# Shared logits groups, FFN column blocks of two and three, later tanh buffers and a new planned order in an attention-and-FFN kernel on one core

## The chip, the cores and the metric

The kernel runs on one core of one Trainium2 chip. The metric is the device time of one launch in microseconds (us). A core has five engines with their own instruction queues, each worked through in order: TensorE (PE, matrix products; its weight loads are shown as PEld), VectorE (DVE), ScalarE (ACT), GpSimd (POOL) and SyncE (SP, here the queue that issues nearly all DMAs). Matrix products write to PSUM, which the kernel holds as one tile `ps` of eight banks of 512 f32 columns; ACT and VectorE read them from there.

## The reference

2048 tokens of width 448, 16 heads of width 28, four segments of 512 tokens. Inside a segment attention is causal; what earlier segments hold comes in through a state M and a normaliser z. After it comes a gated FFN of width 1792. Both halves sit in residual branches with a layer norm, and a conditioning vector gives shifts, scales and gates.

```python
for s in range(N):                       # N = 4 segments of L = 512
    logits = einsum('bhqd,bhkd->bhqk', qs, ks) * scale + mask      # causal
    a_dot = einsum('bhqk,bhkd->bhqd', softmax(logits), vs)
    a_mem = (phi(qs) @ M) / (phi(qs) @ z + 1e-06)
    outs.append(g * a_mem + (1.0 - g) * a_dot)
    M = M + einsum('bhld,bhle->bhde', phi(ks), vs); z = z + sum(phi(ks))
...
mod = (silu(c) @ w_mod).reshape(...)     # sa, ca, ga, sb, cb, gb
h = layernorm(x) * (1 + ca) + sa
x = x + ga * A(h)                        # attention, then @ wo
h = layernorm(x) * (1 + cb) + sb
x = x + gb * ((sigmoid(h @ w_gate) * (h @ w_up)) @ w_down)
```

## The kernel before

**Stages.** The kernel runs once over four segments. For each one: a first layer norm and its transposition (`ln1`), the q, k and v products (`proj`, L665 and L686, evicted by ACT at L673 and L690), attention in four units of four heads each, the state update (`memory`), the output projection with residual and second norm (`wo_ln2`), and the FFN (`ffn`). Work of different segments overlaps.

**One attention unit.** Four heads lie in four quarters of PE's rows, so four products of 28 rows run side by side ("R" mode). The keys are taken in four blocks of 128; because of the causal mask block kb needs only the queries from kb x 128 on, 512, 384, 256 and 128 columns. They are gathered into three logits groups, each in four PSUM banks, one bank per head: block 0 (512 columns), blocks 1 and 3 (384 + 128), block 2 (256, half-filled). ACT makes one exponential of each group into the buffer `pT` (L755), POOL zeroes the upper triangle of each diagonal block (L761), and the product with v (L769, "C" mode, 32 columns of PE per head) accumulates all four blocks. There are two `pT` buffers; a unit takes one with its first logits group and gives it up after L769. After it come 32x32 transposes and normalisation on VectorE (L776 to L817). From segment 1 on the state's product (L783) is added; phi(q) and phi(k) start with an exponential on ACT (L697). phi(k) is transposed by a DMA (L708) and goes into the state product of `memory` (L714).

**The second norm.** L831 multiplies by wo (whose columns are scaled by ga beforehand), VectorE adds it to x (L835), takes statistics, POOL computes the reciprocal deviation (L574), VectorE normalises (L582), four DMAs transpose (L592), and ACT and VectorE apply shift and scale (L602, L605). Then the FFN of that segment can start.

**The FFN.** Width 1792 is 14 columns of 128. For each column, gate and up products go into a bank each. The contraction over 448 rows has three chunks of 128 and one of 64. A column taken alone makes 8 full-array matmuls, its last chunk padded with zeros. In a block of two columns the 64-row chunks of gate and up run side by side in the upper and lower half of PE's rows (L856, "R" mode): the first column's three chunks, the half-height products of both columns, then the second column's three chunks, which go on accumulating. Segment 0 takes 14 columns alone, the others 7 blocks of two (`REST`). ACT takes tanh of the gate into `tt` (L882, two buffers), VectorE combines it with up (L885) into one of 18 `fT` buffers; then L895 multiplies by w_down, whose 14 blocks were scaled by gb before (L551; blocks from `wdd` on by POOL, the others by VectorE).

**Order.** Nothing is issued in the order in which it is written. Every piece of work is a node with an engine, an estimated duration, dependencies, buffers it takes and uses, and a priority. `Graph.run` plays the nodes through with these estimates: at each moment every free engine takes the ready node of highest rank plus priority whose buffers are free, and the order found is what is emitted into the queues. A switch of PE's mode (`mode`: F whole array, R and C divided) costs the plan 100 ns. `Graph.fill` puts dummy matmuls (L930, L933) where the plan has PE idle in the first 90 us. `PRM` holds the priorities; the planned slot of a node decides its place, while on the chip only real dependencies and buffer releases are waited for.

Of the kernel before, what the change touches and what calls it, by code (L numbers as in the profile page):

```python
# [13 lines left out]
P = 128  # L14
# [4 lines left out]
FILL = 450  # L19


PRM = dict(T0=5000, STEP0=-1500.0, STEP=10000.0, lg=76000, ex=15000, mask=49000, wo=79000, tanh=-15500,
           up=81000, f=175500, dn=-495800, phi=-82000, t=-80000, ln1_1=-17000, ln1_2=-57000, ln1_3=-52000,
           mem=-32000, pj_0=36000, pj_1=5000, pj_2=-43000, pj_3=9000, ot=399000, stall=300, wds=-42000,
           wos=144000, wdd=6, mod=-26000, a0=99000, w0=-36000, stay=120000)


class Slot:
# [16 lines left out]
class Graph:  # L45
# [24 lines left out]
        return n  # L70

    def ready_at(self, n):
        t = n.release
        if n.move is not None and len(self.landed) >= LANES:
            t = max(t, self.landed[-LANES])
        for d in n.deps:
            t = max(t, d.end + d.lag + (self.LAG[d.eng][n.eng] if d.eng in self.LAG else 0))
        return t

    def ranks(self):  # L80
# [29 lines left out]
    def run(self):  # L110
# [3 lines left out]
        avail = {e: [] for e in ENGINES}  # L114
        for n in self.nodes:
            if not n.deps:
                avail[n.eng].append(n)
        at = dict.fromkeys(ENGINES, 0.0)
        mode = None
# [3 lines left out]
        while done < len(self.nodes):  # L123
            moved = False
            for e in ENGINES:
                if at[e] > t:
                    continue
                ready = sorted((n for n in avail[e] if self.ready_at(n) <= t), key=lambda n: -(n.rank + n.prio + (PRM["stay"] if e == "PE" and n.mode != "F" != mode else 0)))
                narrow = None
                for n in ready:  # L130
                    if n.lock is not None and self.port - t - n.lock > PRM["stall"]:
                        continue
                    got = self.place(n, t, narrow)
                    if got is None:
                        if narrow is None and any(s.width > 1 for s in n.take):
                            free = self.free["bank"]
                            narrow = min((0, 1), key=lambda h: sorted(free[4 * h:4 * h + 4], reverse=True))
                        continue
                    for s, i in zip(n.take, got):
                        s.at, s.t0 = i, t  # L140
                        for w in range(s.width):
                            self.free[s.pool][i + w] = float("inf")
                    extra = 0
                    if e == "PE":
                        extra = SWITCH if n.mode != mode else 0
                        mode = n.mode
                    n.start = t
                    if n.lock is not None:
                        extra = max(0.0, self.port - t - n.lock)
                    n.end = t + n.dur + extra  # L150
                    if n.lock is not None:
                        self.port = n.end
                    at[e] = n.end
                    if n.move is not None:
                        self.ring = max(self.ring, n.end) + n.move
                        n.lag = self.ring - n.end + LAND
                        self.landed.append(n.end + n.lag)
                    avail[e].remove(n)
                    order.append(n)
                    done += 1  # L160
                    for s in {id(x): x for x in (*n.take, *n.use)}.values():
                        if all(u.end is not None for u in s.users):
                            f = max(u.end + (u.lag if u.move is not None else 0) for u in s.users) + 120
                            for w in range(s.width):
                                self.free[s.pool][s.at + w] = f
                            if s.pool == "bank":
                                s.t1 = f
                                self.used.append(s)
                    for o in n.outs:
                        left[id(o)] -= 1  # L170
                        if left[id(o)] == 0:
                            avail[o.eng].append(o)
                    moved = True
                    break
            if moved:
                continue
            times = [x for x in at.values() if x > t]
            times += [r for e in ENGINES for n in avail[e] if (r := self.ready_at(n)) > t]
            times += [x for x in (self.port - PRM["stall"], self.port) if x > t]
            times += [x for x in self.landed if x > t]  # L180
            times += [f for fs in self.free.values() for f in fs if t < f < float("inf")]
            assert times, "the graph cannot go on"
            t = min(times)
# [24 lines left out]
def kernel(  # L208
# [31 lines left out]
    EPS = 1e-5  # L240
    OFF = (0, L, 2 * L, 2 * L - P)
    PTW = 2 * L + 2 * P
    KB_GROUPS = ((0,), (1, 3), (2,))
    NWARM = 12
    MOD_ACT = ((1, 3), (1, 3))

    REST = ((1,) * 14, (2,) * 7, (2,) * 7, (2,) * 7)
    NXN, NH, NQ, NV, NPT, NFT = 6, 3, 3, 3, 2, 18

    x_dram = A_x[0]  # L250
# [476 lines left out]
            rm_n[(s + 1, hc)] = dve(260, lambda hc=hc, rm=rm: nc.vector.tensor_tensor(  # L727
                rm_r[:, rm.at, :], M_sb[:, hc, :], bmask[:, s, :], ALU.mult), [u, n_bmask], take=[rm], lock=0, prio=PRM["mem"])

    def attention(s, hc, oT, release, prev):  # L730
        q, k, v = qT_of[s], kT_of[s], vt_of[s]
        pT = Slot("pT")
        a0 = 0 if s else PRM["a0"]
        masks = []
        for g, kbs in enumerate(KB_GROUPS):
            lg = Slot("bank", 4)
            w0 = OFF[kbs[0]]
            wid = sum(L - kb * P for kb in kbs)

            def mm(kbs=kbs, lg=lg):  # L740
                o = 0
                for kb in kbs:
                    nq = L - kb * P
                    for hs in range(4):
                        r = slice(HP * hs, HP * hs + Dh)
                        nc.tensor.matmul(ps[:, lg.at + hs, o:o + nq], lhsT=kT_r[r, k.at, hc, kb * P:(kb + 1) * P],  # L746
                                         rhs=qT_r[r, q.at, hc, kb * P:L], start=True, stop=True,
                                         tile_position=(HP * hs, 0))
                    o += nq
            n = add("PE", 230 if wid == L else 120, mm, [q_n[(s, hc)], k_n[(s, hc)], *lg_prev],  # L750
                    take=[lg, pT] if g == 0 else [lg], use=[q, k], release=release(g), mode="R", prio=PRM["lg"] + a0)
            lg_n.setdefault((s, hc), n)

            def ex(lg=lg, w0=w0, wid=wid):
                nc.scalar.activation(pT_r[:, pT.at, :, w0:w0 + wid], ps[:, lg.at:lg.at + 4, 0:wid], AF.Exp, scale=scale)  # L755
            e = act(1765 if wid == L else 920, ex, [n], use=[lg, pT], prio=PRM["ex"] + a0)
            lg_prev[:] = [n, e]
            for kb in kbs:
                def mask(kb=kb):
                    blk = pT_r[:, pT.at, :, OFF[kb]:OFF[kb] + P]  # L760
                    nc.gpsimd.affine_select(out=blk, in_=blk, compare_op=ALU.is_ge, fill=0.0, base=0,  # L761
                                            pattern=[[0, 4], [1, P]], channel_multiplier=-1)
                masks.append(pool_op(610, mask, [e], prio=PRM["mask"] + a0, use=[pT], lock=0))
        acc, A, R, O = bank(), Slot("A"), Slot("R"), Slot("O")

        def pv():
# [76 lines left out]
    def ffn(s, hT, hs):  # L843
# [15 lines left out]
        for size in REST[s]:  # L859
# [6 lines left out]
            for i, f in enumerate(fcs):  # L866
                if i == lead:
                    n_rest = gu_prev[0] = add("PE", size * 216, lambda fcs=fcs, bs=bs, lead=lead: rest(fcs, bs, lead),
                                              [gu_prev[0]], take=[x for g in fcs[lead:] for x in bs[g]],
                                              use=[hT, *(x for g in fcs[:lead] for x in bs[g])], mode="R",  # L870
                                              prio=PRM["up"])
                for j, (w_sb, loads, other) in enumerate(((wg_sb, lg_, tts[f]), (wu_sb, lu_, fs[f]))):
                    late, b = i >= lead, bs[f][j]
                    n = gu_prev[0] = add("PE", (4 if whole else 3) * 216,
                                         lambda w_sb=w_sb, b=b, f=f, whole=whole, late=late: half(w_sb, b, f, whole, late),
                                         [*hs, *loads, *n_gpad, gu_prev[0]], take=[other] if late else [b, other],
                                         use=[hT, b] if late else [hT], mode="F", prio=PRM["up"] * j)
                    done[f, j] = n
            for i, f in enumerate(fcs):
                g, u = (n_rest, n_rest) if i < lead and not whole else (done[f, 0], done[f, 1])  # L880
                (gp, up), tt, ft = bs[f], tts[f], fs[f]
                a = act(500, lambda gp=gp, tt=tt: nc.scalar.activation(tt_r[:, tt.at, :], pf(gp), AF.Tanh, scale=0.5), [g],  # L882
                        use=[gp, tt], prio=PRM["tanh"])
                fts.append(ft)
                fns.append(dve(605, lambda up=up, tt=tt, ft=ft: nc.vector.scalar_tensor_tensor(  # L885
                    fT_r[:, ft.at, :], tt_r[:, tt.at, :], 1.0, pf(up), op0=ALU.add, op1=ALU.mult), [a, u, *wm_done],
# [30 lines left out]
    for s in range(NSEG):  # L917
        oT = Slot("oT")
        on = []
        for hc in range(NHC):  # L920
            on.append(attention(s, hc, oT, lambda g, i=s * NHC + hc: pace(i + g / 3.0), on[-1] if on else None))
        if s + 1 < NSEG:
            memory(s)
        ffn(s, *wo_ln2(s, oT, on))
# [40 lines left out]
```

## Time and profile before

| | us |
|---|---|
| median of 8 runs | 254.21 |
| lowest, highest | 252.36, 256.69 |
| profiled execution | 256.62 |
| its span, first to last instruction | 254.9 |
| PE, DVE, ACT, POOL busy in the span | 242.5, 184.8, 157.3, 98.4 |
| mean granted PE clock | 0.993 |

The page names instructions by engine and line: `PE ps L848` is a matmul at line 848 that writes `ps`. A group of instructions shows its busy time, the mean of one in ns, and the idle time just before them with what ended most of it. Three groups that matter here:

```profile
L755 ACT ACTIVATE pT<-ps 128x2048 bf16<-128x2048 f32 (+1 forms) x48 | 77.5, 1614 | 17.7 <-PE ps L746 16.5
L761 POOL TENSOR_SCALAR_AFFINE_SELECT pT<-pT 128x512 bf16<-128x512 bf16 x64 | 43.8, 696 | 65.2 <-ACT pT L755 65.2
L882 ACT ACTIVATE tt<-ps 128x512 f32<-128x512 f32 x56 | 33.4, 599 | 50.6 <-PE ps L856 36.7
```

The first is the exponentials of the logits, 48 of them in two forms; the shapes apart, the 32 whole ones take 1895 ns and the 16 half ones 1052 ns in the mean. The second is the causal masks, one per diagonal block; POOL mostly waits for the exponential. The third is the tanh of the FFN.

### The profile page before, as it was taken

To read this page: it belongs to the slowest core of one execution; us is meant where nothing else is said; L and a number is where in the kernel's file an instruction comes from. 1 tells how busy PE (TensorE), PEld (TensorE's weight loads), DVE (VectorE), ACT (ScalarE), POOL (GpSimd) and SP (SyncE) were. 2 spreads that over 40 slices of the span, in tenths; PEclk is the share of its full clock that TensorE was granted. 3 is DMA by queue.
4 is the path that set the end of the run, shared out by engine and by line. 5 is a ranking of instruction groups with operands and counts; after the bars stand their busy time and mean duration, and the time that the engine had idled before them with its cause. 6 is when DMAs were issued, how large, how long until landed. Compare 5 with 4: busy or idle time off the path is not lost.

```text
span 254.9 us, 4553 instructions
## 1 busy us (share of the span) xinstructions
PE 242.5 (95%) x1665; PEld 104.9 (41%) x1665; DVE 184.8 (73%) x413; ACT 157.3 (62%) x202; POOL 98.4 (39%) x162
## 2 busy tenths in 40 slices
PE   7997996999989999999899999999999999999994
PEld 2543443534433443444344334344433445334351
DVE  7659765667998889998999889962866882454223
ACT  2588999699999989889865734554542232313210
POOL 7728654387844237572436343411311220000000
PEclk9999999799999999999999999999999999999999
DMA  6999999610052101013210100310100022100002
GB/s 184 231 300 225 297 313 215 67 21 0 3 103 43 23 0 23 0 21 67 41 24 0 54 3 0 78 22 3 54 21 1 0 41 44 36 24 13 3 0 72
DMA packets 27966, 16.99 MB, mean 67 GB/s; under 512 B 18472, under 2 KB 26600, under 8 KB 27944
## 3 DMA queue, kind: packets, MB, share of 16 engines
q1 hardware_dynamic: 27416, 16.08, 27.0%
q10 hardware_dynamic: 528, 0.63, 0.8%
q8 instruction: 13, 0.21, 0.4%
q14 instruction: 9, 0.07, 0.1%
HBM read 10.67 MB, written 1.84 MB: 49 GB/s over the span
## 4 chain that ended last, share of the span: by engine, by line
PE 62%; DVE 4%; DMA 3%; ACT 1%; issue 1%; DVEq 0%; ACTq 0%
PE ps L848 31%; PE ps L895 16%; PE ps L856 4%; PE ps L831 4%; PE ps L746 3%; DMA hT<-xn 2%; PE ps L769 2%; PE ps L665 1%; DVE ot L901 1%; PE ps L783 1%; DMA out_dram<-ot 1%; ACT hT L602 1%; DVE A L776 1%; ACT pT L755 0%; DVE U L813 0%
## 5 line engine op out<-in xcount | busy, mean ns | idle before, releaser
L755 ACT ACTIVATE pT<-ps 128x2048 bf16<-128x2048 f32 (+1 forms) x48 | 77.5, 1614 | 17.7 <-PE ps L746 16.5
L761 POOL TENSOR_SCALAR_AFFINE_SELECT pT<-pT 128x512 bf16<-128x512 bf16 x64 | 43.8, 696 | 65.2 <-ACT pT L755 65.2
L882 ACT ACTIVATE tt<-ps 128x512 f32<-128x512 f32 x56 | 33.4, 599 | 50.6 <-PE ps L856 36.7
L885 DVE SCALAR_TENSOR_TENSOR fT<-tt,ps 128x512 bf16<-128x512 f32 x56 | 38.0, 682 | 28.1 <-ACT tt L882 24.2
L848 PE MATMUL ps<-hT,wg_sb 128*128 128x512 bf16 x182 | 48.9, 381 | 0.2
L848 PE MATMUL ps<-hT,wu_sb 128*128 128x512 bf16 x182 | 48.5, 379 | 0.0
L895 PE MATMUL ps<-wd_sb,fT 128*128 128x448 bf16 x224 | 46.3, 353 | 0.5 <-DVE A L776 0.5
L895 PEld LDWEIGHTS <-fT 128*128 128x128 bf16 x224 | 21.5, 98 | 21.9 <-issue 1.5
L848 PEld LDWEIGHTS <-wu_sb 128*128 128x128 bf16 x182 | 17.1, 98 | 21.2 <-issue 1.2
L848 PEld LDWEIGHTS <-wg_sb 128*128 128x128 bf16 x182 | 15.5, 97 | 23.8 <-issue 9.9
L566 DVE BATCH_NORM_STATS2 st<-x_sb 128x6 f32<-128x448 bf16 x32 | 19.5, 610 | 4.1 <-DMA x_sb<-in_A_x_dram 4.0
L776 DVE STREAM_TRANSPOSE A<-ps 128x512 f32<-128x512 f32 x28 | 19.2, 700 | 4.0 <-PE ps L769 3.2
L901 DVE TENSOR_TENSOR ot<-ps,x_sb 128x448 bf16<-128x448 f32 x16 | 10.0, 623 | 13.3 <-PE ps L895 12.2
L582 DVE TENSOR_SCALAR xn<-x_sb,mv,rs 128x448 bf16<-128x448 bf16 (+1 forms) x48 | 16.4, 395 | 4.2 <-DMA hT<-xn 2.5
L746 PE MATMUL ps<-qT,kT 28*128 28x512 bf16 (+3 forms) x256 | 17.6, 302 | 1.8 <-ACT pT L755 1.3
L815 POOL TENSOR_TENSOR O<-U 128x448 bf16<-128x448 f32 x12 | 13.7, 1144 | 13.3 <-DVE U L813 13.3
L665 PE MATMUL ps<-hT,wq_sb 128*128 128x512 bf16 x64 | 16.5, 380 | 0.3 <-ACT pT L755 0.3
L665 PE MATMUL ps<-hT,wk_sb 128*128 128x512 bf16 x64 | 16.5, 380 | 0.0
L574 POOL TENSOR_TENSOR rs<-rs,mhalf 128x1 f32<-128x1 f32 (+1 forms) x23 | 15.0, 652 | 1.9
L700 DVE TENSOR_TENSOR pq<-e 128x512 bf16<-128x512 bf16 x24 | 12.2, 510 | 1.7 <-PE ps L783 0.6
L813 DVE TENSOR_TENSOR U<-A,R 128x896 f32<-128x896 f32 x12 | 13.4, 1113 | 0.2
L686 PE MATMUL ps<-wv_sb,hT 128*128 128x448 bf16 x64 | 13.5, 353 | 0.0
(104 smaller groups left out, 293.3 us busy)
## 6 DMA issues: line engine op xcount, KB each, us to landing
out_dram<-ot SPq DMA_DIRECT2D x16, 112.0 KB, 1.7
fT<-in_w_mod_dram SPq DMA_DIRECT2D x1, 1568.0 KB, 14.7
x_sb<-in_A_x_dram SPq DMA_DIRECT2D x3, 448.0 KB, 7.0
wg_sb<-in_B_w_gate_dram SPq DMA_DIRECT2D x3, 448.0 KB, 6.2
wu_sb<-in_B_w_up_dram SPq DMA_DIRECT2D x3, 448.0 KB
wd_sb<-in_B_w_down_dram SPq DMA_DIRECT2D x2, 448.0 KB, 10.4
wd_sb<-in_B_w_down_dram SPq DMA_DIRECT2D x2, 336.0 KB, 10.0
pT<-in_w_mod_dram ACTq DMA_DIRECT2D x1, 392.0 KB
```

Of the source, the lines that this page charges most:

```text
L566: nc.vector.bn_stats(st_r[:, st.at, :], src)
L574: nc.gpsimd.tensor_tensor(r, r, mhalf[:, 0:w], ALU.pow)
L582: nc.vector.tensor_scalar(dst, x, mv_r[:, mv.at, t, 0:1], rs_r[:, mv.at, t:t + 1], op0=ALU.subtract, op1=ALU.mult)
L665: nc.tensor.matmul(pf(b), lhsT=w_sb[:, kc, hc * 4:(hc + 1) * 4, :].rearrange("p h e -> p (h e)"), rhs=hT_r[:, hT.at, kc, :], start=(kc == ...
L746: nc.tensor.matmul(ps[:, lg.at + hs, o:o + nq], lhsT=kT_r[r, k.at, hc, kb * P:(kb + 1) * P], rhs=qT_r[r, q.at, hc, kb * P:L], start=True, ...
L755: nc.scalar.activation(pT_r[:, pT.at, :, w0:w0 + wid], ps[:, lg.at:lg.at + 4, 0:wid], AF.Exp, scale=scale)
L761: nc.gpsimd.affine_select(out=blk, in_=blk, compare_op=ALU.is_ge, fill=0.0, base=0, pattern=[[0, 4], [1, P]], channel_multiplier=-1)
L776: nc.vector.transpose(A_r[:, A.at, i, :, :].rearrange("p b e -> p (b e)"), pf(b))
L848: nc.tensor.matmul(pf(b), lhsT=w_sb[:, k, fc * P:(fc + 1) * P], rhs=hT_r[:, hT.at, k, :], start=(k == 0 and not late), stop=(k == n - 1 an ...
L882: a = act(500, lambda gp=gp, tt=tt: nc.scalar.activation(tt_r[:, tt.at, :], pf(gp), AF.Tanh, scale=0.5), [g], use=[gp, tt], prio=PRM["tanh"])
L885: fns.append(dve(605, lambda up=up, tt=tt, ft=ft: nc.vector.scalar_tensor_tensor(fT_r[:, ft.at, :], tt_r[:, tt.at, :], 1.0, pf(up), op0=AL ...
L895: nc.tensor.matmul(pf(b)[:, 0:D], lhsT=fT_r[:, fts[fc].at, t * P:(t + 1) * P], rhs=wd_sb[:, fc, :], start=(fc == 0), stop=(fc == NFC - 1))
```

## The change

- Logits are now made for two units at a time (`logits`). The half-filled groups (block 2) of both share one group: five groups for two units where there were six. The shared group takes the second unit's `pT` buffer, and its exponential writes into both buffers. `attention` begins at the product with v.
- `REST` comes from `PRM`: segment 0 takes 10 columns alone and 2 blocks of two, segment 1 has 7 alone, two blocks of three and a last one alone, segment 2 has 7 blocks of two, segment 3 has four blocks of three and one of two. A block of three runs two columns' full chunks, three columns' half-height products, then the third column's chunks.
- The planner lets tanh take its `tt` buffer when it starts; before, the gate's matmul took it. The half-height products have a mode of their own, "Q". A rule can hold back a single divided-array node for up to `hQ` = 100 ns after it is ready. Ready times are computed once.
- All priorities are new, and `wdd` goes from 6 to 11: VectorE scales 11 blocks of w_down, POOL 3.

```diff
-           mem=-32000, pj_0=36000, ..., stall=300, wds=-42000,
-           wos=144000, wdd=6, mod=-26000, a0=99000, w0=-36000, stay=120000)
+           mem=-16000, pj_0=31000, ..., stall=200, wds=-8000,
+           wos=201000, wdd=11, mod=-18000, a0=96000, w0=-36000, stay=123000, hR=0, hC=0, hQ=100, whole_0=10,
+           group_0=2, whole_1=7, group_1=3, whole_2=0, group_2=2, whole_3=0, group_3=3)
...
-                ready = sorted((n for n in avail[e] if self.ready_at(n) <= t), key=lambda n: -(n.rank + n.prio + ...))
+                ready = [n for n in avail[e] if self.ready_at(n) <= t]
+                if e == "PE":
+                    tiled = [n for n in ready if n.mode != "F"]
+                    if mode == "F" and len(tiled) == 1 and self.ready_at(tiled[0]) + PRM["h" + tiled[0].mode] > t:
+                        ready.remove(tiled[0])
...
-    REST = ((1,) * 14, (2,) * 7, (2,) * 7, (2,) * 7)
+    REST = []
+    for g in range(NSEG):
+        n, size = PRM[f"whole_{g}"], PRM[f"group_{g}"]
+        REST.append((1,) * n + (size,) * ((NFC - n) // size) + (((NFC - n) % size,) if (NFC - n) % size else ()))
...
-    def attention(s, hc, oT, release, prev):
-        pT = Slot("pT")
-        for g, kbs in enumerate(KB_GROUPS):
+    def logits(s, hcs, release):
+        q, k = qT_of[s], kT_of[s]
+        u, w = hcs
+        pT, masks = {u: Slot("pT"), w: Slot("pT")}, {u: [], w: []}
+        for g, items in enumerate((((u, 0),), ((u, 1), (u, 3)), ((u, 2), (w, 2)), ((w, 0),), ((w, 1), (w, 3)))):
             lg = Slot("bank", 4)
+            shared = items[0][0] != items[-1][0]
...
+            n = add("PE", 230, mm, [x for hc, _ in items for x in (q_n[(s, hc)], k_n[(s, hc)])] + lg_prev,
+                    take=[lg, pT[u]] if g == 0 else [lg, pT[w]] if g == 2 else [lg], ...)
+            def ex(items=items, lg=lg, shared=shared):
+                w0 = OFF[items[0][1]]
+                if shared:
+                    dst = pT_r[:, :, :, w0:w0 + L // 2]
+                    src = ps[:, lg.at:lg.at + 4, :].rearrange("p h (n w) -> p n h w", n=2)
+                else:
+                    dst, src = pT_r[:, pT[items[0][0]].at, :, w0:w0 + L], ps[:, lg.at:lg.at + 4, :]
+                nc.scalar.activation(dst, src, AF.Exp, scale=scale)
+            e = act(1765, ex, [n], use=[lg, *slots], prio=PRM["ex"] + a0)
...
-                for j, (w_sb, loads, other) in enumerate(((wg_sb, lg_, tts[f]), (wu_sb, lu_, fs[f]))):
+                for j, (w_sb, loads, other) in enumerate(((wg_sb, lg_, []), (wu_sb, lu_, [fs[f]]))):
...
                 a = act(500, lambda gp=gp, tt=tt: nc.scalar.activation(tt_r[:, tt.at, :], pf(gp), AF.Tanh, scale=0.5), [g],
-                        use=[gp, tt], prio=PRM["tanh"])
+                        take=[tt], use=[gp], prio=PRM["tanh"])
...
-        for hc in range(NHC):
-            on.append(attention(s, hc, oT, lambda g, i=s * NHC + hc: pace(i + g / 3.0), on[-1] if on else None))
+        for hc in range(0, NHC, 2):
+            lgs = logits(s, (hc, hc + 1), lambda g, i=s * NHC + hc: pace(i + g * 0.4))
+            for u, (pT, masks) in lgs.items():
+                on.append(attention(s, u, oT, pT, masks, on[-1] if on else None))
```

## The prediction

> **What bounds the kernel now.** I read the page's busy table first, then the slices, then windows cut at the places where the slices change, then the chain of waits inside those windows. The first lines say that TensorE (PE) has no room: it is busy for 95% of the span. The two rows of slices under them (forty equal slices, tenths) say that it is not alone: from about 20 to 80 us ScalarE (ACT) is as full as PE.
>
> ```profile
> PE 242.5 (95%) x1665; PEld 104.9 (41%) x1665; DVE 184.8 (73%) x413; ACT 157.3 (62%) x202; POOL 98.4 (39%) x162
> ...
> PE   7997996999989999999899999999999999999994
> ...
> ACT  2588999699999989889865734554542232313210
> ```
>
> The windows separate the stages. A row gives the stretch and its length, then busy time and count of PE, PEld, VectorE (DVE), ACT and GpSimd (POOL), then the granted clock. The third and fourth rows, from the first FFN matmul at 78.4 us to the last matmul, have PE busy for 170.1 of 171.3 us: there the end moves only if PE gets less work, or loses the remaining 1.2 us of stalls. The second row is the opposite case: ACT is busy for 29.71 of 29.90 us and PE idles 1.6 us; besides, that PE time holds 11 filler matmuls (L933), 11 x 0.216 = 2.4 us of nothing. The first row is a hole with a lowered clock.
>
> ```profile
> 44.00:48.50 4.50, 4.01 (x32) 2.38 (x36) 2.19 (x6) 2.20 (x5) 0.03 (x1) 0.62 0.70 111
> 48.50:78.40 29.90, 28.29 (x235) 12.27 (x228) 25.57 (x59) 29.71 (x40) 20.81 (x29) 1.00 0.21 34
> 78.40:127.50 49.10, 48.42 (x359) 20.03 (x359) 44.37 (x98) 43.01 (x51) 24.06 (x35) 1.00 0.13 26
> 127.50:249.70 122.20, 121.65 (x728) 51.48 (x728) 79.47 (x156) 48.92 (x61) 26.17 (x40) 1.00 0.09 22
> ```
>
> The chain of waits (start, duration, what) shows how the ACT stage ends. The last transposed block of segment 0's second norm has landed at 75.64, but ACT first finishes two phi exponentials that stand ahead of it, then does its two modulations, and the FFN starts when they end. ACT's queue opens the FFN, not the DMA.
>
> ```profile
> 73.22 2.42 DMA hT<-xn
> ...
> 75.77 0.70 ACT e L697 x2
> ...
> 76.80 1.58 ACT hT L602 x2
> ...
> 78.43 1.67 PE ps L848 x7
> ```
>
> Further down the same chain prices one FFN block of two columns. Six full-array matmuls take 1.29 after other full-array work, four half-height ones 0.54 (two run at a time, so 2 x 0.216 + 0.11), and the next six 1.40: each change between whole and divided array costs 0.11 us.
>
> ```profile
> 168.59 1.29 PE ps L848 x6
> 169.88 0.54 PE ps L856 x4
> 170.42 1.40 PE ps L848 x6
> ```
>
> Two rows of ACT's timeline give the exponentials: 1.09 long for half a group with the next start 0.91 later, 1.94 for a whole one with the next start 1.76 later. PE's timeline shows the hole at 44: it waits for the first transposed phi(k), and the later `rep` product runs at the lowered clock.
>
> ```profile
> 72.15 1.09 ACT L755 ACTIVATE pT<-ps 128x1024 bf16<-128x1024 f32 x1
> ...
> 74.01 1.94 ACT L755 ACTIVATE pT<-ps 128x2048 bf16<-128x2048 f32 x1
> ```
>
> ```profile
> 43.97 0.40 PE L714 MATMUL ps<-vt,pk 128*128 128x128 bf16 x4 [2.08 <-DMA pk<-pq]
> ...
> 46.32 1.70 PE L474 MATMUL ps<-fT,silu_bc 112*128 112x448 bf16 x4
> ```
>
> **What the Trainium skill says.** "TensorEngine Tiling (Array Packing)", Key Properties: changing the tiling mode drains TensorE, using another tile of the same mode does not. The trace agrees, 0.11 us a change. "TensorE: Matmul & The Clock Gate", Part 1, has back-to-back warm 512-column matmuls 215.7 ns apart; here 1.29 / 6 = 0.215. "ScalarE: Activation LUTs", What ACT_TABLE_LOAD costs: an ACTIVATE without pointer operands takes 186 ns + 0.833 ns per element, and neighbours overlap by 93 ns; that is 1892 and 1039 ns for 2048 and 1024 elements, and the groups' means are 1895 and 1052. So joining two halves saves about 0.09 us by that page; by starts it is 2 x 0.91 - 1.76 = 0.06, and I take 0.07.
>
> **The change, part by part.** A planner in the kernel decides every queue's order, so beside the diff I compared how the instructions of the two built programs stand on each engine.
>
> *Shared exponential.* Per pair of units six logits groups become five: 48 to 40 in all, the same 256 matmuls. ACT: 8 x 0.07 = 0.6 us less. The new operand reads and writes in eight rows of 256, which the trace does not show: at worst it costs two halves, 1.84 (the gain is gone), at best 1.76. I take 1.77. PE: eight groups fewer, each entered and left through a mode change.
>
> *FFN blocks.* A column alone costs 8 x 0.216 = 1.73, in a pair (1.29 + 0.54 + 1.40) / 2 = 1.62, in a triple (18 x 0.216 + 3 x 0.216 + 0.22) / 3 = 1.58. Before: 14 alone, 21 pairs. After: segment 0 has 10 alone and 2 pairs, segment 1 has 8 alone and 2 triples, segment 2 has 7 pairs, segment 3 has 4 triples and a pair: 18 alone, 10 pairs, 6 triples. 92.0 us before, 91.9 after: nothing. Segment 1 even pays +0.65. What counts is how often PE changes mode in the whole order. From the first FFN matmul on I count 110 changes before and 89 after; 21 x 0.11 = 2.3 us less, against four more matmul slots, 4 x 0.216 = 0.9 us. One state product (0.2 us) now stands ahead of the FFN. So PE has 2.3 - 0.9 + 0.2 = 1.6 us less from there to the end.
>
> *Tanh buffers.* Tanh waits for VectorE's release of its buffer in both programs; only the planner's account changes. No cost by itself; it acts through the order.
>
> *Scaling W_down.* Five of the 14 products move from POOL (5 x 1.16 = 5.8 us less) to VectorE (5 x 0.38 = 1.9 us more). Six of VectorE's eleven now stand before segment 0's first residual add, where it was idle for 2.69 us at 55 to 58; five stand between the last norm and the modulation, where it waits for four transposes (about 4 us) and has by my count 4.1 us to do. So they just fit; were the cover gone, they would cost 5 x 0.35 = 1.8 us.
>
> *Order up to the FFN.* ACT decides. Before, from the end of the exponential at 55.20 to the modulation at 76.80 I count 5 whole and 2 half exponentials, 8 casts of q or k, 6 of v, 6 phi exponentials and 2 modulations: 5 x 1.77 + 2 x 0.92 + 8 x 0.47 + 6 x 0.43 + 6 x 0.52 + 2 x 0.72 = 21.6, exactly the gap, so the count is good. After, the same stretch holds 6 whole exponentials, 8, 5, 5 and 2: 20.6. Ahead of it stand only two exponentials of segment 0 and three casts, 4.9 us, where before 6.7 us passed (48.49 to 55.20). With the modulations of 1.5 us the FFN starts 27.0 us after that stage's first exponential, not 29.9: 2.9 gained. But that exponential comes later. Its logits now stand behind an attention product and two fillers on PE (0.65 + 0.54 = 1.2 us), and the wait at 44 is now for two transposed phi(k) instead of one; on SyncE's queue the second takes the place of an hT transpose whose landing VectorE saw at 44.4 instead of 44.0, so 0.4 more. Net 2.9 - 1.6 = 1.3 us. Bounds: 2.9 if the fillers and the second transpose cost nothing, 0 if VectorE, which then waits for a later hT transpose ahead of freeing PE's banks, adds 1.3 (one transpose is 1.2 on that queue).
>
> *Order after it.* Before, PE loses 1.2 us to late segment starts and banks (122, 127, 144 us). After, 14.8 us of PE work lie between the end of segment 1's output projection and its first FFN matmul, where the chain before took 109.6 to 122.1, 12.5 us: no stall. For segments 2 and 3 the cover is 14.0 and 13.4 against 12.8 and 13.9 for the same chain before: enough, and just short by 0.5. I take 0.6 of the 1.2 as regained; bounds +1.2 and -2.
>
> Sum: 1.3 + 1.6 + 0.6 = 3.5 us. On the profiled execution (256.62 us, span 254.9) that gives 253.1; that execution is 2.4 above the median of 254.21, partly its clock hole, so I apply the difference to the median: 250.7 us.
>
> **Rivals.** *Slower: the pT pair.* The shared exponential writes both pT buffers, so it waits for the attention product of the previous pair's second unit. Between that unit's last exponential and the shared one stand two exponentials, 3.5 us; before there were two and a half, 4.5 us. Two masks (2 x 0.63 + 0.2) and the product (0.65) need 2.1, which leaves 1.4 us for queueing on PE, and FFN blocks now stand up to 16 matmuls (3.5 us) together. Where the product stands behind such a block, ACT stalls by up to 2.1 us and the logits stop PE. At a mean of 0.9 over seven pairs: 6.3 - 3.5 = 2.8 us slower, 257.0. It decides from 0.5 us per pair on. Against it: in the new order I find the products of units 5 to 7 placed after their masks should be done.
>
> *No change.* The new order around 44 us eats the earlier FFN start, tight segment ends eat the 0.6 and some more, and the rest of the PE gain shows: 1.0 us, 253.2. For it speaks that ACT and PE are both full there, so each late item costs.
>
> *More.* Fillers and transposes cost nothing and all stalls go: 2.9 + 1.6 + 1.2 = 5.7 us, 248.5.
>
> **How the numbers follow.** Forecast 0.58, more 0.12, no change 0.13, slower 0.17. A measurement of this kernel can tell about 0.5%, 1.3 us, from no change: 252.9 to 255.5. Forecast and "more" are faster except for 0.02 of the forecast's upper edge; "no change" gives 0.05 to faster and 0.08 to same; "slower" leaves 0.03 within the band: faster 0.73, same 0.13, slower 0.14. The range runs from below "more" (247.8, with 0.7 for a segment start or clock hole that disappears) to 255.0, which leaves out most of the slower case.
>
> **What would show it.** Right: the first FFN matmul (now L876) at about 77 us with ACT without gaps before it; 40 exponentials of one form near 1.89 us; PE idle after that of 1 us or less; 133 mode changes in all instead of 159. Wrong: ACT waiting for POOL or PE ahead of the shared exponential at each pair, PE waiting for ACT ahead of logits inside the FFN, a PE hole of over 4 us at 42 to 48, or waits of the half-height matmuls for banks in segments 1 and 3.

## The result, and the profile after

| | before | after |
|---|---|---|
| median | 253.43 us (32 runs, 252.0 to 259.9) | 249.23 us (11 runs, 248.17 to 252.1) |
| ratio after/before | | 0.9845, 95% interval 0.9818 to 0.9872 |
| profiled execution, span | 256.62, 254.9 | 249.09, 247.1 |
| granted PE clock in it | 0.993 | 1.0 |

The change makes the kernel 1.55% faster, which is 3.9 us of 253.43; the forecast was 3.5. The two profiled executions lie 7.8 us of span apart, because the recorded execution of before was a late one. Readings below therefore use a second look at before, `c_before2` (253.0 us, span 251.3). All ratios count only the runs within 1.5% of the fastest of their kernel; the recorded execution of before, and that of `blocks_old` below, lie outside.

First the page of after: the line of busy times and the slices of PE and ACT (forty, in tenths).

```profile
PE 238.0 (96%) x1661; PEld 104.7 (42%) x1661; DVE 186.7 (76%) x418; ACT 154.9 (63%) x194; POOL 95.9 (39%) x157
...
PE   7999978999989999999999999999999999999994
...
ACT  2589979999999897188988746544712132222300
```

PE is busy for 4.5 us less than in the page of before (242.5), and for 3.8 less than in the second look (241.8). After the twelfth slice, which ends at 74 us, no digit of PE is below 9 until the last slice. The groups of exponentials and masks:

```profile
L778 ACT ACTIVATE pT<-ps 128x2048 bf16<-128x2048 f32 x40 | 75.7, 1893 | 14.4 <-PE ps L761 13.3
L784 POOL TENSOR_SCALAR_AFFINE_SELECT pT<-pT 128x512 bf16<-128x512 bf16 x64 | 46.9, 746 | 65.8 <-ACT pT L778 65.8
```

Forty exponentials of one form, mean 1893 ns: the eight shared ones, with their rows of 256, cost what a whole group costs. The windows of after, by stage (stretch, length, busy time and count of PE, PEld, DVE, ACT, POOL, then clock, DMA share and GB/s):

```profile
40.00:48.00 8.00, 7.07 (x71) 3.55 (x70) 7.03 (x19) 7.87 (x11) 4.26 (x6) 1.00 0.46 93
48.00:77.00 29.00, 27.74 (x224) 11.90 (x223) 26.39 (x68) 29.00 (x39) 15.05 (x24) 1.00 0.19 39
77.00:125.00 48.00, 47.77 (x345) 20.41 (x345) 44.36 (x96) 37.57 (x45) 24.77 (x33) 1.00 0.12 23
125.00:242.00 117.00, 117.00 (x724) 50.60 (x717) 75.74 (x150) 50.09 (x60) 26.23 (x41) 1.00 0.09 23
```

The hole at 44 us with its lowered clock is gone. In the second row ACT is busy for all of 29.00 us, as in the stage before it. In the last row PE idles for nothing at all, where the second look at before loses 0.55 us from 125 us on:

```profile
125.00:247.50 122.50, 121.95 (x730) 51.59 (x728) 79.61 (x155) 48.03 (x61) 26.14 (x40) 1.00 0.09 23
```

The chain of waits of after, where the ACT stage ends and the FFN opens:

```profile
71.70 0.73 DVE hT L617 x2
72.43 0.64 DVE A L804
73.07 0.04 issue
73.11 2.97 PE ps L876 x13
```

VectorE, not ACT, is named last here: it finishes its half of the modulation, then empties one attention bank (L804), and the first FFN matmul takes that bank. ACT's two modulations run from 71.91 to 73.46, so the two engines arrive together.

Cut at the first FFN matmul, the spans read (us):

| | first FFN matmul | from there to PE's end | rest | span |
|---|---|---|---|---|
| before, second look | 74.4 | 173.1 | 3.8 | 251.3 |
| after | 73.1 | 170.2 | 3.8 | 247.1 |
| gain | 1.3 | 2.9 | 0.0 | 4.2 |

The count of PE's work after the first FFN matmul, from the order of the built programs, is 171.15 before and 169.53 after. So the 2.9 are 1.6 of work and 1.3 of stalls (1.9 before, 0.6 after). "Stalls" here is the time less the counted work; the idle time that the windows show is smaller, 0.9 and 0.2.

### The profile page after: what moved, and what is told of

Read it like the earlier page. It is cut to its first block, busy times and chain, and to the rows that moved or that the text cites. A ratio compares the mean times of both kernels' runs of the same rounds, so it can differ in the third digit from the quotient of the medians.

```text
span 247.1 us, 4534 instructions
## 1 busy us (share of the span) xinstructions
PE 238.0 (96%) x1661; PEld 104.7 (42%) x1661; DVE 186.7 (76%) x418; ACT 154.9 (63%) x194; POOL 95.9 (39%) x157
## 4 chain that ended last, share of the span: by engine, by line
PE 66%; DMA 2%; DVE 2%; issue 0%; DVEq 0%
PE ps L876 34%; PE ps L923 15%; PE ps L884 4%; PE ps L859 4%; PE ps L761 3%; PE ps L677 3%; PE ps L797 2%; DMA hT<-xn 2%; PE ps L811 1%; DMA out_dram<-ot 1%; DVE hT L617 1%; DVE A L804 1%; DVE ot L929 1%; PE ps L726 0%; DVE rm L739 0%
## 5 line engine op out<-in xcount | busy, mean ns | idle before, releaser
L778 ACT ACTIVATE pT<-ps 128x2048 bf16<-128x2048 f32 x40 | 75.7, 1893 | 14.4 <-PE ps L761 13.3
L784 POOL TENSOR_SCALAR_AFFINE_SELECT pT<-pT 128x512 bf16<-128x512 bf16 x64 | 46.9, 746 | 65.8 <-ACT pT L778 65.8
L910 ACT ACTIVATE tt<-ps 128x512 f32<-128x512 f32 x56 | 32.6, 598 | 54.4 <-PE ps L884 40.0
L913 DVE SCALAR_TENSOR_TENSOR fT<-tt,ps 128x512 bf16<-128x512 f32 x56 | 37.3, 678 | 21.2 <-ACT tt L910 18.6
L876 PE MATMUL ps<-hT,wu_sb 128*128 128x512 bf16 x186 | 49.3, 379 | 0.0
L876 PEld LDWEIGHTS <-wu_sb 128*128 128x128 bf16 x186 | 18.2, 98 | 21.8
L876 PEld LDWEIGHTS <-wg_sb 128*128 128x128 bf16 x186 | 16.2, 98 | 23.7 <-issue 8.3
L804 DVE STREAM_TRANSPOSE A<-ps 128x512 f32<-128x512 f32 x28 | 19.2, 699 | 3.5 <-PE ps L797 2.7
L761 PE MATMUL ps<-qT,kT 28*128 28x512 bf16 (+3 forms) x256 | 15.9, 300 | 1.0 <-ACT pT L778 0.8
L712 DVE TENSOR_TENSOR pq<-e 128x512 bf16<-128x512 bf16 x24 | 12.9, 536 | 4.8 <-ACT e L709 3.4
L585 POOL TENSOR_SCALAR rs<-mv 128x1 f32<-128x1 f32 (+1 forms) x23 | 5.4, 236 | 21.7 <-DVE mv L579 21.7
```

The lines of the kernel that those rows point to most:

```text
L778: nc.scalar.activation(dst, src, AF.Exp, scale=scale)
L804: nc.vector.transpose(A_r[:, A.at, i, :, :].rearrange("p b e -> p (b e)"), pf(b))
L876: nc.tensor.matmul(pf(b), lhsT=w_sb[:, k, fc * P:(fc + 1) * P], rhs=hT_r[:, hT.at, k, :], start=(k == 0 and not late), stop=(k == n - 1 an ...
```

## Experiments

Twelve runs were made besides before and after. "Counted work" is TensorE's work after the first FFN matmul, from the emitted order. The first six change one thing in a fixed order or repeat a kernel; the last six change the nodes, so the planner orders everything anew.

### Was the recorded execution of before a bad one? (`c_before`, `c_before2`)

Before, unchanged, one look each.

> The kernel before, unchanged, profiled once more. Its recorded span is 7.8 us longer than that of the changed kernel, while the timed ratio 0.9845 is worth 3.9 us. Theory that the recorded execution of before was a bad one: span near 251, the w_mod product at L474 starting near 24 instead of 25.8, the wait for phi(k) at L714 shorter than 1 us, no lowered clock. Rival, that the transposes and loads come late by the kernel's own order: span near 254, the product again at 25.8 and the wait again about 2 us.

Measured: 254.71 us, span 253.0, clock 0.993, first FFN matmul at 75.3. Part of the distance went, the lowered clock did not: the span lies between the two that were expected, and so does the wait ahead of L714, 1.44 us.

> The kernel before, unchanged, a second look. Nothing is left out. Theory (about half of its executions lower TensorE's clock after the wait for the first transposed phi(k) at 42 to 44 us, which costs some 1.4 us): the span is either near 251.0 with a granted clock of 1.0, or near 252.5 with 0.993 and a rep product (L474) well above 1.0 us. Rival (the lowered clock belongs to some chips or to late loads, not to that wait): the clock of this look says nothing about where the wait stands.

Measured: 253.0 us, span 251.3, clock 0.993: the span of one expected case with the clock of the other. PE's timeline in this look (start, duration, what, and in brackets the idle time before it):

```profile
39.52 0.29 PE L746 MATMUL ps<-qT,kT 28*128 28x256 bf16 x4
40.53 0.40 PE L714 MATMUL ps<-vt,pk 128*128 128x128 bf16 x4 [0.72 <-DMA pk<-pq]
40.76 0.39 PE L634 MATMUL ps<-ident,xn 128*128 128x128 bf16 x4
41.63 0.83 PE L634 MATMUL ps<-ident,xn 128*128 128x128 bf16 x12 [0.48 <-DVE M_sb L721]
42.61 1.52 PE L474 MATMUL ps<-fT,silu_bc 112*128 112x448 bf16 x4
```

Two waits of 0.72 and 0.48 us, for the transposed phi(k) and for VectorE, and the `rep` product right behind them takes 1.52 us instead of 0.92. So in this execution even these short waits go with a lowered clock. The Trainium skill, "TensorE: Matmul & The Clock Gate", Part 1, has the clock fall back after at least one idle window of about 3.4 us; the waits here are much shorter, and the measurement decides.

### Fill the wait (`b_fill`)

Before, with eight full matmuls that write the waiting product's own bank ahead of it:

```diff
+                if s == 0 and hc == 0:
+                    w = wq_sb[:, 0, :, :].rearrange("p h e -> p (h e)")
+                    for _ in range(8):
+                        nc.tensor.matmul(pf(b), lhsT=w[:, 0:P], rhs=w, start=True, stop=True)
```

> The kernel before with eight 512-column matmuls (8 x 0.216 = 1.7 us, their results are overwritten) put on TensorE directly ahead of the state products that wait for the first transposed phi(k) at 42 to 44 us; nothing is left out. Theory (the idle wait lowers the clock in half of the runs): granted clock 1.0 in nearly all runs, median about 0.7 us lower than before, ratio 0.997. Rival 1 (the clock is lowered by something else): the ratio stays at 1.000. Rival 2 (the wait was no spare time, the products are in the way): up to 1.7 us slower, ratio up to 1.007.

Measured: 252.08 us over 22 runs, ratio 0.9995 (0.9969 to 1.0021). The windows of `c_before2` and then of `b_fill`, 36 to 48 us:

```profile
36.00:48.00 12.00, 10.55 (x88) 5.10 (x86) 8.16 (x22) 10.43 (x16) 5.84 (x8) 0.86 0.82 135
```

```profile
36.00:48.00 12.00, 11.55 (x107) 5.86 (x105) 9.25 (x22) 11.04 (x17) 5.87 (x8) 1.00 0.84 148
```

The clock does what the theory says: 21 of 22 runs have 0.997 or more. Of the 22 runs of before that the comparison counts, 12 do (median 251.86), and 10 have 0.993 or less (253.69). The ratio itself can't tell 0.997 from 1.000. So shown is that eight full matmuls in the wait keep the clock up, not that this speeds the program up; the distance of 1.8 us between the two sets of runs is an association. Whether the wait itself or the small products around it lower the clock was not separated. In the run group of `e_exp2`, 13 runs of before at 0.997 or more have a median of 252.6, against 249.2 there at the same clock: 3.4 us of the gain (4.0 by that group's ratio) are there without any lowered clock.

### Price of a mode change (`e_modes`)

After, with the third w_down product of each part of four in segments 2 and 3 split into four 32-column products, 48 mode changes more in the same order:

```diff
+                        if fc == f0 + 2 and s >= 2:
+                            for hs in range(4):
+                                r = slice(hs * HP, (hs + 1) * HP)
+                                nc.tensor.matmul(pf(b)[r, 0:D], lhsT=fT_r[:, fts[fc].at, t * P + hs * HP:...],
+                                                 rhs=wd_sb[:, fc, :], ..., tile_position=(0, HP * hs))
...
```

> The changed kernel, with the third of the five (or four) w_down products of each part split into four 32-column tiles in segments 2 and 3: 24 products, 48 mode changes more, the same columns streamed. My theory (0.11 us a change, nothing hides it once TensorE is the bound): 48 x 0.11 = 5.2 us slower than the changed kernel, about 254.4. Rival (changes are hidden, the gain came from elsewhere): within 1 us of the changed kernel, 249 to 250.

Measured: 254.34 us, ratio to before 1.0031 (1.0007 to 1.0054), span 252.2 against 247.1: 5.1 us for 48 changes, 0.106 each. PE is busy for all of the stretch (125 to 247 us):

```profile
125.00:247.00 122.00, 122.00 (x790) 48.99 (x790) 75.88 (x150) 50.08 (x60) 26.23 (x42) 1.00 0.09 22
```

The price that the forecast of 2.3 us for 21 changes rests on holds, and added PE work goes into the end in full.

### The shared exponential in two halves (`e_exp2`)

After, in the same order, the shared group's exponential issued once for each unit:

```diff
-                nc.scalar.activation(dst, src, AF.Exp, scale=scale)
+                if shared:
+                    for i in range(2):
+                        nc.scalar.activation(dst[:, i], src[:, i], AF.Exp, scale=scale)
...
```

> The changed kernel in the same order, the shared exponential issued as two halves of 1024 elements. My theory: ScalarE pays 0.07 us for each of eight, three of them ahead of the first FFN matmul: 0.2 us, 249.4, the first FFN matmul 0.2 later; ratio to the changed kernel 1.001. Rival (the joined exponential is what saves): 0.5 us or more, since ScalarE is full until 73 us.

Measured: 249.22 us, ratio 0.9841 (0.9798 to 0.9885), as after. Joining the exponentials saves nothing that the program's time can show; the interval leaves room for the 0.6 us of the forecast. ACT's timelines do show a price: from the start of a shared exponential to the next start it is 1.77 us joined and 1.82 in two halves (means over the eight), so 0.05 each, 0.4 of ACT in all. From the opening exponential of segment 1's stage to the first FFN matmul both take 26.6 us; only one shared exponential lies in that stretch.

### Without the later fillers (`e_nofill`)

```diff
-    G.fill(90000, dummy)
+    G.fill(20000, dummy)
```

> The changed kernel in the same order without the seven filler matmuls after 20 us. I charged two of them, 0.43 us, to the logits that open the stage at 46 us. Theory: the exponential there starts 0.3 to 0.4 earlier, the FFN too, 248.9. Rival: nothing, since the hT modulation on ScalarE ahead of it decides, 249.2; or slower by up to 1 us if TensorE's clock falls in the gaps.

Measured: 250.19 us, ratio 0.9869 (0.9815 to 0.9923). The logits that open the stage of segment 1 start at 46.07 in place of 45.98. PE's timeline of after, then of `e_nofill`:

```profile
45.17 0.61 PE L963 MATMUL ps<-wq_sb 128*128 128x512 bf16 x2
45.98 0.40 PE L761 MATMUL ps<-qT,kT 28*128 28x512 bf16 x4 [0.20 <-ACT hT L654]
```

```profile
46.07 0.40 PE L761 MATMUL ps<-qT,kT 28*128 28x512 bf16 x4 [0.73 <-ACT hT L654]
```

Without the two fillers PE just waits longer for ACT, so they cost nothing. They also seem to keep the clock up: of the five runs without them that the comparison counts, three had 0.993 or less; none of the eleven of after was below 0.997. But the fastest of the five, 248.46, is one of the three, so a price of that clock is not shown here.

### One part of the change at a time (`share_only`, `order_only`)

`share_only` is before with the new `logits` function and its five groups; `order_only` is before with the planner rule, mode "Q" and all new priorities, but six groups:

```diff
+        for g, items in enumerate((((u, 0),), ((u, 1), (u, 3)), ((u, 2),), ((w, 0),), ((w, 1), (w, 3)), ((w, 2),))):
```

> The kernel before with the shared group and exponential alone: FFN blocks, planner, priorities and tanh buffers as before. Nothing is left out. Theory (the gain is TensorE work after the first FFN matmul, counted from the order: 12 mode changes and two matmul slots fewer there, 1.5 us, and 0.6 us of ScalarE ahead of it at most): 1.5 to 2.1 us faster, ratio 0.992 to 0.994. Rival (the shared exponential, which waits for both pT buffers, stalls ScalarE when the order isn't fitted to it): slower than before, ratio above 1.000.

Measured: 257.31 us, ratio 1.018 (1.0132 to 1.0228). The count was right, PE has 169.64 us of work after the first FFN matmul, but that matmul comes at 79.1 instead of 74.4, and 3.7 us of stalls follow in place of 1.9.

> The kernel before with the new planner rule and the new priorities alone: six logits groups to a pair of units, FFN blocks of one and two as before, tanh buffers taken on TensorE as before. Nothing is left out. Theory (work from the order: 1.8 us less on TensorE after the first FFN matmul, but no ScalarE time saved ahead of it): 1.0 to 2.0 us faster, ratio 0.992 to 0.996. Rival 1 (the whole gain is the order): as the full change, ratio 0.985. Rival 2 (an order fitted to five groups only hurts with six): ratio 1.000 or above.

Measured: 260.96 us, ratio 1.0307 (1.0257 to 1.0357). First FFN matmul at 81.6, stalls of 6.3 us after it, with 169.32 us of work. Either part alone is slower than before, so the gain is not a sum of the parts. The expected mechanism for `share_only` (ACT stalled by the wait for both `pT` buffers) is not what happened: of the 18.4 us that ACT idles ahead of exponentials there, 1.0 is for a mask. In after it is one wait of 0.8, in the view of that line (what ended ACT's idle time before it, us and times):

```profile
  PE ps L761: 13.3, 14
  POOL pT L784: 0.8, 1
```

In `share_only` PE stops ahead of logits at 27 us for 2.6 us (VectorE's hT) and at 48 us for 1.8 us (an exponential), both ahead of the FFN; the second look at before has no such stops there, and behind the first one two products run slowly (1.89 and 1.57 us in place of 1.03). So the lateness most likely belongs to the new order; the shared group in before's own order was not tried.

### One part taken back (`split6`, `blocks_old`, `blocks_tt_old`, `wdd6`)

After with six groups to a pair; with the FFN blocks of before; with these blocks and the tanh buffer taken by the gate matmul; with six W_down blocks on VectorE:

```diff
-        for g, items in enumerate((((u, 0),), ((u, 1), (u, 3)), ((u, 2), (w, 2)), ((w, 0),), ((w, 1), (w, 3)))):
+        for g, items in enumerate((((u, 0),), ((u, 1), (u, 3)), ((u, 2),), ((w, 0),), ((w, 1), (w, 3)), ((w, 2),))):
```

```diff
-           ... wdd=11, ..., whole_0=10, group_0=2, whole_1=7, group_1=3, whole_2=0, group_2=2, whole_3=0, group_3=3)
+           ... wdd=11, ..., whole_0=14, group_0=2, whole_1=0, group_1=2, whole_2=0, group_2=2, whole_3=0, group_3=2)
```

```diff
-                for j, (w_sb, loads, other) in enumerate(((wg_sb, lg_, []), (wu_sb, lu_, [fs[f]]))):
+                for j, (w_sb, loads, other) in enumerate(((wg_sb, lg_, [tts[f]]), (wu_sb, lu_, [fs[f]]))):
```

```diff
-           wos=201000, wdd=11, ...
+           wos=201000, wdd=6, ...
```

> The changed kernel with six logits groups to a pair of units instead of five; its planner rule, priorities, FFN blocks and tanh buffers stay, and the planner orders the six groups anew. Nothing is left out. Theory A (the five groups are worth their own work: 8 x 0.07 us of ScalarE, and 0.9 us of TensorE after the first FFN matmul by the count of the order, 170.39 against 169.53): 1.0 to 1.5 us slower than the changed kernel, ratio to before 0.988 to 0.991. Theory B (the order fits one set of operations, and every other set loses several us, as it did with either part alone): ratio 1.000 or above. Which term grows tells them apart further: under A stalls after the first FFN matmul stay at 0.6 us, under B they grow to 2 us and more, or the FFN starts after 75 us.

> The changed kernel with the FFN blocks of before (segment 0: 14 columns alone, the other segments 7 pairs each), all else as changed. Nothing is left out. The count of TensorE's work after the first FFN matmul is the same, 169.53 us (eight mode changes more, fewer matmul slots). Theory A (the blocks themselves are worth nothing): as the changed kernel, ratio to before 0.984 to 0.987. Theory B (the order fits one set of operations only): ratio 1.000 or above, the loss being stalls.

> The same with FFN blocks of before, and in addition the tanh buffer taken by the gate matmul as before. Nothing is left out. Work after the first FFN matmul 169.75 us, two mode changes more than with those blocks alone. Theory A (where the buffer is taken changes nothing but the planner's account): within 0.5 us of the kernel with the old blocks alone. Theory B (the order fits one set of operations only): ratio 1.000 or above, and off from that kernel by over 1 us either way. Rival (the gate matmul really waited for the buffer): 1 to 2 us slower than with the old blocks alone, and matmuls of the gate wait for VectorE's releases inside the FFN.

> The changed kernel with six of the W_down scalings on VectorE instead of eleven, as many as before (the others on GpSimd). Nothing is left out. The planner then has 167.48 us of TensorE work after the first FFN matmul, 2.05 less, but 5.3 us more ahead of it, 16 fillers (3.5 us) among it. Theory A (the moved scalings were free, and the fillers fill waits): the FFN starts at 74 to 75 us, total as the changed kernel within 1 us, ratio 0.982 to 0.989. Theory B (the order fits one set of operations only): ratio 0.995 or above.

Measured, with the earlier ones (us; the hole is PE's wait for segment 3's second norm, ahead of that segment's FFN; a dash marks what was not read):

| kernel | ratio to before | first FFN matmul | counted work | last exponential ends | hole |
|---|---|---|---|---|---|
| before (`c_before2`) | 1 | 74.4 | 171.2 | 183.5 | none |
| after | 0.9845 | 73.1 | 169.5 | 179.0 | none |
| `share_only` | 1.018 | 79.1 | 169.6 | 187.3 | none |
| `order_only` | 1.031 | 81.6 | 169.3 | 193.2 | none |
| `split6` | 1.054 (1.048 to 1.061) | 72.3 | 170.4 | 203.4 | 10.5 |
| `blocks_old` | 1.034 (1.027 to 1.041) | - | 169.5 | - | - |
| `blocks_tt_old` | 1.077 (1.070 to 1.083) | 73.0 | 169.8 | 210.3 | 9.6 |
| `wdd6` | 1.059 (1.054 to 1.065) | 80.5 | 167.5 | 205.6 | 10.3 |

All four are far slower than before, though none of them has more counted work than before and `wdd6` has 3.7 us less. `wdd6` missed its expectation ahead of the FFN too, 80.5 where 74 to 75 was written. `split6` is the clearest: its FFN starts earlier than after's, and it still loses 17.3 us of span to after. PE's timeline of `split6`:

```profile
202.21 3.01 PE L924 MATMUL ps<-wd_sb,fT 128*128 128x448 bf16 x15
205.15 0.73 PE L798 MATMUL ps<-pT,vt 128*32 128x512 bf16 x16
206.03 2.43 PE L924 MATMUL ps<-wd_sb,fT 128*128 128x448 bf16 x12 [0.16 <-issue]
208.30 0.73 PE L860 MATMUL ps<-wo_sb,oT 128*128 128x448 bf16 x3
212.11 2.63 PE L860 MATMUL ps<-wo_sb,oT 128*128 128x448 bf16 x13 [3.08 <-DVE oT L846]
225.23 1.44 PE L877 MATMUL ps<-hT,wg_sb 128*128 128x512 bf16 x3 [10.49 <-DVE hT L617]
```

The last attention product (L798) runs at 205, and by 208.5 the FFN of segment 2 has nothing left. The chain of waits of `split6` (its longest pieces) shows what PE then waits for:

```profile
209.30 1.01 DVE U L842
210.44 1.14 POOL O L844
214.01 1.04 DVE x_sb L864 x2
218.19 1.64 DVE xn L594 x6
219.82 0.98 SPq L604
220.90 1.22 SPq L604
222.20 2.44 DMA hT<-xn
```

Normalising, output projection, residual, statistics, norm, transposes: some 22 us from the last exponential (203.4) to the first FFN matmul of segment 3 (225.2), nearly all of it on other engines and on DMAs (PE's share after that exponential is the 0.7 of L798, the 3.4 of L860, and what was left of segment 2's FFN). The windows of `split6` also show a lowered clock behind the hole (the clock is the third number from the end: 0.61 in the hole, 0.60 for 6.8 us behind it):

```profile
214.74:225.20 10.46, 0.00 (x1) 0.11 (x1) 5.40 (x18) 0.45 (x1) 2.83 (x7) 0.61 0.25 50
225.20:232.00 6.80, 6.77 (x21) 2.20 (x22) 0.74 (x2) 2.14 (x4) 0.00 (x0) 0.60 0.01 2
```

In after the same chain is no shorter (last exponential at 179.0, first FFN matmul at 206.5), but FFN work of segment 2 lies over it to the last moment. PE's timeline of after:

```profile
202.07 0.81 PE L876 MATMUL ps<-hT,wu_sb 128*128 128x512 bf16 x3
202.72 3.95 PE L923 MATMUL ps<-wd_sb,fT 128*128 128x448 bf16 x20
206.50 0.81 PE L876 MATMUL ps<-hT,wg_sb 128*128 128x512 bf16 x3
```

What follows: the part taken back isn't what costs 13 to 23 us against after (ratios 1.034 to 1.077 less 0.985). In the three traces of the table the same priorities, with another set of nodes, put the end of segment 3's attention 24 to 31 us later, behind the FFN that should have covered its end. The worth of the blocks, the tanh buffers and the moved W_down scaling, each by itself in the new order, was thus not measured, nor were they tried in after's frozen order. Theory B of these expectations stands, with the limit that each kernel was planned once; why the planner's choices tip so far was not traced.

## Why the prediction was right

**Mode changes and matmul slots, 1.6 us.** Right. 0.11 us a change was measured on purpose, and the count of 1.6 is the work part of the 2.9 that disappear after the first FFN matmul.

**The FFN start, 1.3 us.** Probably too large; that the second look shows just this number (74.4 to 73.1) is in part luck. First, the mark: the matmul at 78.43, which the forecast calls the first of the FFN, is the fourth. The first starts at 77.43, and the fourth waits for the last part of the modulation. The first four in the recorded execution, in the second look, with the wait filled (`b_fill`), and after:

```profile
77.43 1.38 PE L848 MATMUL ps<-hT,wg_sb 128*128 128x512 bf16 x4
```

```profile
74.43 1.38 PE L848 MATMUL ps<-hT,wg_sb 128*128 128x512 bf16 x4
```

```profile
73.48 1.38 PE L852 MATMUL ps<-hT,wg_sb 128*128 128x512 bf16 x4
```

```profile
73.11 1.02 PE L876 MATMUL ps<-hT,wg_sb 128*128 128x512 bf16 x4 [0.28 <-DVE A L804]
```

The fourth of them starts at 75.43 in the second look, 74.48 in `b_fill` and 73.76 after. So the forecast's mark moved by 1.7 us against the second look, but by 0.7 against an execution of before with the clock up: about 1 us is the lowered clock, which the sum did not have. The "77" named as a sign was tied to the recorded execution, whose stage opened late (48.49; 44.77 in the second look, 44.58 in `b_fill`).

The step inside the sum is nearly right: from the opening exponential to that matmul it is 29.9 us in the recorded execution and in `b_fill`, and 27.3 after, 2.6 shorter where 2.9 were worked out. The opening exponential, at 46.48, came 1.9 later than in `b_fill`, where 1.6 were worked out, but for another reason. The fillers charged with 0.54 cost nothing. ACT's timeline of after has the cause:

```profile
41.24 1.95 ACT L778 ACTIVATE pT<-ps 128x2048 bf16<-128x2048 f32 x1
43.01 0.61 ACT L702 CAST vt<-ps 128x448 bf16<-128x448 f32 x1
43.42 1.22 ACT L709 ACTIVATE e<-kT 128x512 bf16<-128x512 bf16 x2
44.47 1.45 ACT L654 ACTIVATE hT<-ps,cols 128x512 bf16<-128x512 bf16 x2
```

A whole exponential, a cast and two phi exponentials now stand ahead of the modulation (L654), which the second look begins at 42.05. The modulation empties the bank that the opening logits need. This step was read from PE's queue, and it is ACT's. How much is left of the net 0.7 is known only roughly: in the four executions with after's order up to there (after, `e_exp2`, `e_nofill`, `e_modes`) the opening lies between 45.6 and 46.7, which makes the net 0.5 to 0.7 in three of them and 1.6 in `e_exp2`.

**Stalls, 0.6 of 1.2.** The forecast's 1.2 was idle time of PE. In that measure the second look has 0.9 and after 0.2: 0.7 regained, close to the forecast. The rest of the 1.3 in the account above, 0.6, lies between busy time and counted work; the wait inside the first four matmuls of before is part of it. The covers of segments 2 and 3, worked out as "enough, and just short by 0.5", sufficed; segment 1, worked out as free of stalls, kept a wait of 0.23 at 119.0, since its chain from the output projection on took 15.1 us and not 12.5.

**Clock.** The forecast mentioned the clock hole only as part of the recorded execution's bad luck and left it out of the sum. It occurs in about half of the runs of before that the comparisons count, so it belongs to the median; with 1.8 us between the two sets, 10 of 22, it is at most about 0.8, and 0.6 by the comparison at the same clock (3.4 of 4.0). So the total is close to the forecast because an FFN start probably taken too large and a clock term left out nearly cancel. To a tenth the split isn't settled, since each trace is one execution.

**Shared exponential, 0.6 us of ACT.** Its form costs nothing extra (1893 ns). By the starts it is 0.4 of ACT and not 0.6; whether it reaches the program's time can't be told: halves in the same order are as fast.

**FFN blocks, tanh buffers, W_down, at nothing.** Not separated, as said. VectorE's cover for W_down, which "just fits", held but for little: PE waits 0.28 us for VectorE ahead of the FFN.

**The rivals.** "The pT pair" would have needed 0.9 us per pair; ACT waited once for a mask, 0.8 us. "No change" fails because only short waits are left at 44 us (0.46 and 0.20) and at the segments' starts (0.23). "More" overstated the FFN start: part of its gain really is eaten by the later opening.

## What to carry to other kernels

Where a planner orders the queues, its priorities and the set of nodes are one thing: of six kernels planned anew with parts in or out, every one was slower than before, by up to several times what the whole change gains. So test a part in the frozen order, and read the count of work from the emitted order. In a PE-bound tail, look first at the last stage's serial chain and at how much work is left to lie over it; it cost some 10 us in the three traces here in which the cover was gone, and the work saved was 1.6. Take the reference for a stage from an execution whose time is near the median.

## What was not expected of the hardware

Waits of PE of 0.72 and 0.48 us within 2 us went with a lowered clock (mean 0.86 over 12 us), and in `e_nofill` waits of 0.50, 0.16 and 0.73 belonged to a program in which three of five runs had it, though the execution with these waits kept 1.0. After a wait of 10.5 us the clock stayed at 0.60 for another 6.8 us, in which seven 512-column matmuls took 3.14 us instead of 7 x 0.216 = 1.5.
